# Attention exponentials: scores computed a second time by key in place of transposed exponentials

## The chip, the cores and the metric

The kernel runs on one core of one Trainium2 chip. The metric is device time in microseconds (us) of one execution. Five engines work side by side, each through its own queue of instructions in order: TensorE (PE in the profile; its weight loads stand apart as PEld), VectorE (DVE), ScalarE (ACT), GpSimd (POOL) and SyncE (SP, whose queue issues most of the transfers between the chip's memories). A score that TensorE computes lands in PSUM, eight banks of 128 partitions x 2 KB; everything else lives in the SBUF or, for long, in device memory (DRAM tiles in the code).

## What is computed

Four layers in a row on x of 2048 x 640: Fourier mixing (A), sliding-window attention (B), A, B, each with a layer norm ahead and a residual. The change is in B alone:

```python
H = 32; Dh = D // H; W = 256
qkv = (x @ wqkv).reshape(B, S, 3, H, Dh) ...
scores = jnp.einsum("bhqd,bhkd->bhqk", q, k) * (Dh ** -0.5)
mask = (idx[:, None] - idx[None, :] >= 0) & (idx[:, None] - idx[None, :] < W)
scores = jnp.where(mask[None, None], scores, -1e9)
p = _softmax(scores, axis=-1)
o = jnp.einsum("bhqk,bhkd->bhqd", p, v)
return o ... @ wo
```

32 heads of 20 features; a query sees itself and the 255 keys before it.

## The kernel before

**Layers.** `spectral` (L292) is layer A, `attention` (L702) layer B; they run as A, B, A, B (L1075 to L1079). Layer A's product over the sequence is one of Strassen's form, with matrices split into two float16 parts; the change doesn't touch it but for the name of the call that issues its matmuls.

**Attention, its loop.** The sequence is cut into 16 tiles of 128 rows and 8 blocks of 256 (QB). A slot `g` (0 to 255, loop at L1034) is one tile of queries `i` and one pair of heads `p`; `place` (L883) orders them, two pairs of heads for each of a block's two tiles by turns. In slot g the program writes, in this order: `scores(g)`, other products (`run_fill`), `exps(g-1)`, `turn(g-2)`, every fourth slot one of the two parts of `values` (lags 7 and 8, VALUE_LAGS) and `back` (lag 9), and more fill. FILL gives how many ns of fill follow: 400 and 620.

**Scores (L888).** Q and K are held transposed, features on partitions: `QS[b]` and `KS[b]`, "stacks" of three float16 parts of 20 features, 60 rows for the first head of a pair (rows 0 to 59) and 60 for the second (from row 64). Four matmuls of 60 rows give 128 queries x up to 384 keys for both heads in `sp`, a PSUM tile of two banks with two buffers. The oldest and the newest 128 keys are then merged under a triangular mask in place (L906), so that 256 columns remain; their maximum is taken (L909, over c0 to 384), scaled (L911), and is the bias of the exponential (L918, ACT, one for each head).

**From query rows to key rows.** The sum over keys needs the exponentials with keys on partitions. `turn` (L922) transposes them by TensorE, four float32 transposes of 128 x 128 (L929) into `ptp`, copies them to the SBUF tile `ptq` by ACT (L935), and POOL zeroes what the window and causality exclude (L938, L940); L938 makes the oldest tile out of the merged one.

**Values and back.** `values` (L947) multiplies V by `ptq` for four heads at once, each in a quarter of TensorE's columns (L961); V has a column of ones per head, so the sum of the exponentials comes with it. DVE copies the result (L966). `back` (L968) turns it to rows (L972), divides by the sum, and splits it in two float16 parts.

**Fill.** The projections of the next block (`proj_qk` L733, `proj_v` L738, products at L275 and L750), the output product of the block before (`out_tile` L795, L806), transposes of 128 columns (L834) and, ahead of the next layer A, its first products (L195) are cut into single matmuls, which `run_fill` (L857) deals out between a slot's steps. `proj.qk` stores each finished piece to DRAM on SP's queue; after the last one of K, and again of Q, `load_stack` (L726) loads the stack of the next block in six transfers. The last tiles' output is summed by parts (`last_out`, L765).

**What sets the order.** Each engine runs its own list in order. The lists are written by a planner from the program's order and a model of times, within the data's dependences; `tc.issue_after(x)` keeps an instruction behind x on its engine. A tile with a tag and `bufs=n` has n buffers in turn: a new one waits until the buffer it gets is released by its last reader. Transfers of SP wait in SP's queue for the buffers and data that they need.

Of the kernel before, what the change touches and what calls it, by code (L numbers as in the profile page):

```python
# [14 lines left out]
OP = mybir.AluOpType  # L15
# [22 lines left out]
LAST_STEPS = (1, 257)  # L38
# [14 lines left out]
def body(ctx: ExitStack, tc: tile.TileContext, x_in, cmat, whid, wqkv, wo, out):  # L53
# [6 lines left out]
    # matrices are held as two float16 parts each  # L60
# [6 lines left out]
    # 1 where a key of the tile two before the query's is still in the window: key > query  # L67
    mask = pers.tile([P, P], I32, name="mask")
    neg = pers.tile([P, P], F32, name="neg")

    def constants():
        make_identity(nc, idf[:])
        nc.vector.tensor_copy(idh, idf)
        nc.gpsimd.memset(mask, 1)
        nc.gpsimd.memset(neg, NEG)
        nc.gpsimd.affine_select(out=mask, in_=mask, pattern=[[1, P]], base=0, channel_multiplier=-1,
                                compare_op=OP.is_gt, fill=0.0)
# [9 lines left out]
    mx_d = dram.tile([1, 2], F32, name="mxd")  # L87

    normed = [None]

    def layer_norm(xs):
        """(x - mean) / sqrt(var + eps), times X_UP, in float32, of some tiles."""
# [48 lines left out]
    # what both kinds of layers hold at some time: the matrix in use with what is read along with it,  # L141
    # and two smaller tiles that pass from the one kind to the other while the rest of it is still at work
# [9 lines left out]
    # parts of z for the seven products, in the order in which they are used  # L152
    B11, T2, B21, T3, T1, T4, B22 = range(7)

    class Hidden:
        """The product over the features, for a tile of the sequence at a time."""
# [20 lines left out]
        def stage(self, s, pool, new=new_f):  # L177
            """Yields the time of each product in ns, and 0 where a set of them is complete."""
# [9 lines left out]
            def product(c, n):  # L188
# [4 lines left out]
                for dt in range(ND):  # L193
                    for l, r in ((0, 0), (0, 1), (1, 0)):
                        self.last = nc.tensor.matmul(z[:, :HD], xt[:, l, dt], w[:, r, c, dt, cs],  # L195
# [43 lines left out]
    def fill_stack(t, b, w):  # L239
        """The three parts of a head's features one below the other, for the products of all their pairs."""  # L240
        for pi in range(2):
            for r, part in enumerate((0, 1, 0) if w == 0 else (0, 0, 1)):
                v = qk_d[b][w][part].rearrange("(p two d) t -> two d p t", two=2, d=DH)[pi]
                r0 = 64 * pi + DH * r
                load(t[r0:r0 + DH], v)

    class Projections:
        """The products with the weights of B, for a block of QB rows at a time."""
# [19 lines left out]
        def qk(self, b, w, ct):  # L268
# [4 lines left out]
            for dt in range(ND):  # L273
                for l, r in ((0, 0), (0, 1), (1, 0)):
                    nc.tensor.matmul(pf[:, :QB], self.w[l][:, dt, cols], xt[:, :, r, dt, :],  # L275
# [12 lines left out]
    # ------------------------------------------------------------------ A  # L288
    # y = [Cr | -Ci] [z_re ; z_im] with z = xn W^T. The product over the sequence is Strassen's, in Winograd's
    # form: rows in pairs of tiles, the inner dimension in its real and imaginary halves, columns in halves of HD.  # L290
    # It is summed in rounds of RS tiles of the sequence.
    def spectral(layer, res_src, hidden, first):  # L292
        with ExitStack() as st:
# [10 lines left out]
            # small pieces of work done beside the main products, one after each of them  # L304
# [36 lines left out]
            def transposed(xs, k, xt):  # L341
                pt = new_f().bitcast(F16)[:, :ND * P].rearrange("p (a b) -> p a b", a=ND)
                for dt in range(ND):
                    nc.tensor.transpose(pt[:, dt], xs[:, k, dt * P:(dt + 1) * P], idh)
# [92 lines left out]
            def product(r, bank, cc, m, start, stop):  # L437
                o = bank[:, :HD]
                n = 0
                for k in range(RS):  # L440
                    zc = hidden.zc[RS * r + k]
                    for a, b in ((0, 0), (0, 1), (1, 0)):
                        nc.tensor.matmul(o, cc[m][:, a, k * P:(k + 1) * P], zc[:, m, b],  # L443
# [87 lines left out]
            # the weights of B: their largest exponent, then the two parts  # L531
# [21 lines left out]
            def b_scale():  # L553
# [5 lines left out]
                nc.tensor.transpose(pt[:2, :P], m2, idf)  # L559
# [545 lines left out]
```

## Time and profile before

| | us |
|---|---|
| three runs | 2437.78, 2438.85, 2439.06 |
| median | 2438.85 |
| span of the profiled execution | 2439.0 |
| first attention layer in it, about | 637 to 1277 |
| second attention layer, about | 1827 to 2439 |

In the profile's groups a row reads: line, engine, operation, output <- inputs, partitions x elements of both, count | busy us, mean ns of one | idle us of the engine just before them and what ended most of it. In the chain a row is start, duration, and whose work it was. L128 is the helper that issues nearly all of SP's transfers.

### The profile page before, as it was taken

The page shows a single profiled execution, that of the slowest core. Times are in us where ns is not written, and L with a number is a line of the kernel's source. Part 1 is how long each engine was busy: PE and PEld are TensorE (multiplying, and loading weights), DVE is VectorE, ACT ScalarE, POOL GpSimd, SP SyncE. Part 2 cuts the span into 40 slices and gives each one's busy share as a digit, 9 for nine tenths or more (in the row PEclk, how much of TensorE's full clock was granted, in tenths as well). Part 3 has the DMA queues.
Part 4 walks back from the last instruction along what each step waited for, and adds up shares of the span by engine and source line. Part 5 has one row for each costly group of instructions (what it writes and reads, how often), then busy time and mean ns, then how long its engine had stood idle before and what let it go on. Part 6 is the DMA issues. An engine that isn't in the chain of part 4 may idle for free.

```text
span 2439.0 us, 53596 instructions
## 1 busy us (share of the span) xinstructions
PE 2314.2 (95%) x20577; PEld 1569.1 (64%) x20577; DVE 1884.4 (77%) x4209; ACT 1357.7 (56%) x2695; POOL 1203.0 (49%) x1448
## 2 busy tenths in 40 slices
PE   7999898987999999999989999999789999999998
PEld 5666576656656666666656777776566666666665
DVE  7888979697778777878877767576967777777776
ACT  5334444433467777777753343443326777777775
POOL 5676757564223333333446867685732233333333
PEclk9999999998999999999999999999999999999999
DMA  5755646274522323232314545355544232322210
GB/s 176 292 198 184 208 149 209 89 250 128 161 64 64 72 75 82 73 78 66 121 67 150 195 137 196 131 190 188 176 142 102 63 70 65 77 66 71 62 44 23
DMA packets 191668, 302.25 MB, mean 124 GB/s; under 512 B 14004, under 2 KB 120756, under 8 KB 182196
## 3 DMA queue, kind: packets, MB, share of 16 engines
q1 hardware_dynamic: 156564, 222.47, 30.9%
q10 hardware_dynamic: 34848, 76.36, 8.3%
q8 instruction: 161, 2.64, 0.4%
q14 instruction: 95, 0.78, 0.1%
HBM read 201.46 MB, written 97.32 MB: 122 GB/s over the span
## 4 chain that ended last, share of the span: by engine, by line
PE 72%; DVE 19%; issue 3%; DMA 3%; ACT 2%; POOL 1%; DVEq 0%; ACTq 0%; SPq 0%; POOLq 0%
PE pf L275 11%; PE ptp L929 9%; PE pv L961 9%; PE pf L195 8%; PE y L443 7%; DVE cc L427 6%; PE pf L750 5%; PE sp L903 5%; PE pf L806 5%; PE z L443 5%; PE x L443 4%; DVE res L450 2%; DVE lnst L98 1%; PE pv L972 1%; PE pf L834 1%
## 5 line engine op out<-in xcount | busy, mean ns | idle before, releaser
L443 PEld LDWEIGHTS <-cc 128*128 128x128 f16 x5376 | 527.9, 99 | 249.6 <-issue 37.2
L918 ACT ACTIVATE pn<-sp,nb,alpha 128x256 f32<-128x256 f32 (+1 forms) x1024 | 516.3, 555 | 100.0 <-DVE nb L911 80.7
L938 POOL TENSOR_SCALAR_AFFINE_SELECT ptq<-ptq 128x512 f32<-128x512 f32 x224 | 142.2, 635 | 591.5 <-ACT ptq L935 591.5
L935 ACT ACTIVATE ptq<-ptp 128x512 f32<-128x512 f32 (+1 forms) x512 | 298.7, 583 | 194.3 <-PE ptp L929 178.2
L275 PE MATMUL pf<-early,big 128*128 128x256 f16 x2400 | 343.6, 277 | 14.0 <-DVE xto L346 13.9
L909 DVE TENSOR_REDUCE m<-sp 128x2 f32<-128x512 f32 (+1 forms) x512 | 343.2, 671 | 11.7
L929 PE MATMUL ptp<-idf,pn 128*128 128x128 f32 x1984 | 314.9, 276 | 3.0 <-ACT ptq L935 0.8
L906 DVE COPY_PREDICATED sp<-mask,sp 128x256 f32<-128x256 int32 x448 | 190.5, 426 | 140.9 <-PE sp L903 131.9
L424 ACT ACTIVATE cc<-cs 128x512 f16<-128x512 f32 x256 | 151.8, 622 | 226.7 <-POOL cs L417 103.3
L443 PE MATMUL y<-zc,cc 128*128 128x320 f16 x1728 | 265.9, 301 | 11.2 <-DVE pf L450 8.1
L275 PEld LDWEIGHTS <-big 128*128 128x128 f16 x2400 | 214.1, 99 | 91.4 <-issue 65.5
L929 PEld LDWEIGHTS ptp<-idf,pn 128*128 128x128 f32 x1984 | 233.3, 141 | 37.1 <-ACT pn L918 8.7
L195 PE MATMUL pf<-big 128*128 128x320 f16 x1680 | 244.6, 301 | 9.4 <-DVE zc L209 6.5
L195 PEld LDWEIGHTS <-big 128*128 128x128 f16 x1920 | 187.5, 99 | 97.7 <-issue 18.9
L961 PE MATMUL pv<-ptq,v 128*32 128x128 f32 (+1 forms) x3840 | 243.4, 333 | 0.2
L427 DVE SCALAR_TENSOR_TENSOR cc<-cs,cc 128x512 f16<-128x512 f32 x256 | 234.6, 930 | 1.6 <-ACT cc L424 1.6
L940 POOL TENSOR_SCALAR_AFFINE_SELECT ptq<-ptq 128x512 f32<-128x512 f32 x256 | 164.0, 641 | 100.5 <-ACT ptq L935 90.6
L427 DVE SCALAR_TENSOR_TENSOR cc<-cq,cc 128x512 f16<-128x512 f32 x192 | 203.8, 1063 | 0.0
L443 PE MATMUL z<-zc,cc 128*128 128x320 f16 x1152 | 180.0, 301 | 8.6 <-DVE res L450 8.6
L443 PE MATMUL x<-zc,cc 128*128 128x320 f16 x1152 | 183.6, 304 | 2.9 <-DVE zc L209 2.9
L750 PE MATMUL pf<-big,early 128*128 128x320 f16 x960 | 170.4, 301 | 0.2
L961 PEld LDWEIGHTS pv<-ptq,v 128*32 128x32 f32 x3840 | 105.5, 109 | 91.1 <-issue 47.8
(136 smaller groups left out, 3565.6 us busy)
## 6 DMA issues: line engine op xcount, KB each, us to landing
cq<-in_cmat_dram SPq DMA_DIRECT2D x64, 1024.0 KB
accd<-res ACTq DMA_DIRECT2D x96, 320.0 KB
res<-accd SPq DMA_DIRECT2D x96, 320.0 KB
qkd<-early SPq DMA_DIRECT2D x160, 128.0 KB
ks<-qkd SPq DMA_DIRECT2D x108, 160.0 KB
qs<-qkd SPq DMA_DIRECT2D x84, 160.0 KB
x2d<-res ACTq DMA_DIRECT2D x32, 320.0 KB
xtd<-xto ACTq DMA_DIRECT2D x32, 320.0 KB
```

Source lines behind the costliest of these rows:

```text
L195: self.last = nc.tensor.matmul(z[:, :HD], xt[:, l, dt], w[:, r, c, dt, cs], start=k == 0, stop=k == 14).ins
L275: nc.tensor.matmul(pf[:, :QB], self.w[l][:, dt, cols], xt[:, :, r, dt, :], start=k == 0, stop=k == 14)
L427: nc.vector.scalar_tensor_tensor(cc[m][:, 1], f, C_UP, cc[m][:, 0], op0=OP.mult, op1=OP.subtract)
L443: nc.tensor.matmul(o, cc[m][:, a, k * P:(k + 1) * P], zc[:, m, b], start=start and n == 0, stop=stop and n == 3 * RS - 1, skip_group_check ...
L750: nc.tensor.matmul(pf[:, :320], proj.rows[b][0][:, ti, l, dt, :], proj.w[r][:, dt, cols], start=k == 0, stop=k == 14)
L906: nc.vector.copy_predicated(sp[:, :, 2 * P:3 * P], mask[:, None, :].to_broadcast([P, 2, P]), far)
L909: nc.vector.tensor_reduce(m, sp[:, :, c0:3 * P], axis=AX.X, op=OP.max)
L918: nc.scalar.activation(pn[:, pi, c0 - P:], sp[:, pi, c0:3 * P], AF.Exp, bias=nb[:, pi:pi + 1], scale=alpha[:, 0:1])
L929: nc.tensor.transpose(pt[:, pi, a], pn[:, pi, a * P:(a + 1) * P], idf)
L935: nc.scalar.activation(q[:, h:h + 2, a0 + 1 + first:a0 + 3], pt[:, :, first:], AF.Copy)
L940: ins = nc.gpsimd.affine_select(out=q[:, :, a0 + 2], in_=q[:, :, a0 + 2], pattern=[[0, 4], [1, P]], base=0, channel_multiplier=-1, compare ...
L961: nc.tensor.matmul(pv[32 * h:32 * h + 32, cols], VS_[kt][:, VS * hh:VS * hh + 32], q[:, h, sel], start=kt == j, stop=kt == j + 1, tile_pos ...
```

## The change

The maxima are still found from scores by query (`scores`, without the scaling L911). But the exponentials are not: the maxima of eight slots (SHARE) are transposed by one small TensorE transpose, split into two float16 parts, stored to DRAM, and loaded as two more rows under each head's 60 rows of Q (`hand_on`). K's stack gets two rows of the constant 2^15 there, loaded from a DRAM tile of ones. A second product of 62 rows with K and Q in the other roles (`by_key`) so gives scores minus maximum, with keys on partitions, for all three tiles of keys, and one ACT instruction writes sigmoid(alpha x - 20) from PSUM to `ptq`; both products and sums of V then carry the same factor. The float32 transposes, their copies and the pairs of exponentials go.

In slot g the order is now: `scores(g)`, `by_key(g-13)`, every fourth slot both parts of `values` (lag 18) and `back` (lag 20), one stretch of fill of FILL[g % 4] ns, and every eighth slot `hand_on` (lag 8; its loads one slot later). Within attention each TensorE instruction is kept behind the one traced before it, so that the planner doesn't move it. `sp` and the new `tp` have two banks and one buffer each (before: `sp` two buffers, `ptp` one bank). The copies of V and of the sums of V pass from DVE to ACT. Both stacks of a block are loaded after the last projection of Q.

```diff
-FILL = (400, 620, 1600)
...
-VALUE_LAGS = (7, 8)
-BACK_LAG = 9
+FILL = (1250, 1450, 300, 1450)
+FILL_END = 1600
...
+SHARE = 8
+HAND_LAG = 8
+KEY_LAG = 13
+VALUE_LAG = 18
+BACK_LAG = 20
+M_UP = 2.0 ** 15
+SHIFT = -20.0
...
+    def tensor(what, *args, **kw):
+        with ExitStack() as order:
+            if in_turn[0] and latest[0] is not None:
+                order.enter_context(tc.issue_after(latest[0]))
+            i = getattr(nc.tensor, what)(*args, **kw)
+        latest[0] = i.ins
+        return i
...
             for r, part in enumerate((0, 1, 0) if w == 0 else (0, 0, 1)):
                 v = qk_d[b][w][part].rearrange("(p two d) t -> two d p t", two=2, d=DH)[pi]
                 r0 = 64 * pi + DH * r
                 load(t[r0:r0 + DH], v)
+            if w:
+                load(t[64 * pi + 3 * DH:64 * pi + 3 * DH + 2], ones_d.rearrange("a (p t) -> a p t", p=NP))
...
             def proj_qk(b, w, ct):
                 yield from proj.qk(b, w, ct)
-                if ct == ND - 1:
-                    load_stack(b, w)
+                if ct == ND - 1 and w == 0:
+                    load_stack(b, 1)
+                    load_stack(b, 0)
...
-                nc.vector.tensor_scalar(o, pf[:, :320].rearrange("p (h e) -> p h e", e=DH), 32.0 / (X_UP * W_UP),
-                                        None, op0=OP.mult)
+                nc.scalar.activation(o, pf[:, :320].rearrange("p (h e) -> p h e", e=DH), AF.Copy,
+                                     scale=32.0 / (X_UP * W_UP))
...
-                sp = ps.tile([P, 2, 512], F32, tag="s", name="sp", bufs=2)
+                sp = ps.tile([P, 2, 512], F32, tag="s", name="sp")
...
-                nc.vector.tensor_reduce(m, sp[:, :, c0:3 * P], axis=AX.X, op=OP.max)
-                nb = sb.tile([P, 2], F32, tag="nb", name="nb", bufs=4)
-                nc.vector.tensor_scalar(nb, m, alpha[:, 1:2], None, op0=OP.mult)
-                SP_[g] = (sp, nb, c0)
+                if g % SHARE == 0:
+                    TOP[g // SHARE] = sb.tile([P, 2, SHARE // 2, 2], F32, tag="m", name="m", bufs=2)
+                nc.vector.tensor_reduce(TOP[g // SHARE][:, i % 2, p % (SHARE // 2)], sp[:, :, c0:3 * P], axis=AX.X, op=OP.max)
+
+            def hand_on(n):
+                b, k = divmod(n, 2 * NP // SHARE)
+                pf = new_f()[:2 * SHARE, :P]
+                transpose(pf, TOP.pop(n).rearrange("p i a b -> p (i a b)"), idf)
+                hl = sb.tile([2 * SHARE, 2, P], F16, tag="hl", name="hl", bufs=2)
+                nc.scalar.activation(hl[:, 0], pf, AF.Copy, scale=-1.0 / M_UP)
+                nc.vector.scalar_tensor_tensor(hl[:, 1], pf, -1.0 / M_UP, hl[:, 0], op0=OP.mult, op1=OP.subtract)
+                load(top_d[n], hl)
+                yield
+                v = top_d[n].rearrange("(i p two) a t -> two a p i t", i=2, two=2)
+                ps_ = slice(SHARE // 2 * k, SHARE // 2 * (k + 1))
                 for pi in range(2):
-                    nc.scalar.activation(pn[:, pi, c0 - P:], sp[:, pi, c0:3 * P], AF.Exp, bias=nb[:, pi:pi + 1],
-                                         scale=alpha[:, 0:1])
+                    r0 = 64 * pi + 3 * DH
+                    for i in range(2):
+                        load(QS[b][r0:r0 + 2, ps_, i * P:(i + 1) * P], v[pi][:, :, i])
...
+            def by_key(g):
...
-                pt = pp.tile([P, 2, 2, P], F32, tag="pt", name="ptp")
-                for pi in range(2):
-                    for a in range(first, 2):
-                        nc.tensor.transpose(pt[:, pi, a], pn[:, pi, a * P:(a + 1) * P], idf)
+                tp = ps.tile([P, 2, 512], F32, tag="t", name="tp")
+                for a in range(first, 3):
+                    kt = i - 2 + a
+                    k0 = (kt % 2) * P
+                    for pi in range(2):
+                        r = slice(64 * pi, 64 * pi + 3 * DH + 2)
+                        matmul(tp[:, pi, a * P:(a + 1) * P], KS[kt // 2][r, p, k0:k0 + P], QS[b][r, p, t0:t0 + P],
+                                         start=True, stop=True)
...
-                nc.scalar.activation(q[:, h:h + 2, a0 + 1 + first:a0 + 3], pt[:, :, first:], AF.Copy)
+                nc.scalar.activation(q[:, h:h + 2, a0 + first:a0 + 3],
+                                     tp[:, :, first * P:3 * P].rearrange("p a (b c) -> p a b c", c=P), AF.Sigmoid,
+                                     bias=shift, scale=alpha[:, 0:1])
...
-                    nc.vector.tensor_copy(PVS[n], pv[:, :2])
+                    nc.scalar.activation(PVS[n], pv[:, :2], AF.Copy)
...
-                run_fill(FILL[0])
-                if 0 <= g - 1 < NG:
-                    exps(g - 1)
-                if 0 <= g - 2 < NG:
-                    turn(g - 2)
+                if 0 <= g - KEY_LAG < NG:
+                    by_key(g - KEY_LAG)
...
-                run_fill(FILL[1])
+                run_fill(FILL[g % 4] if g < NG else FILL_END)
+                n, m = divmod(g - HAND_LAG, SHARE)
+                if m == 0 and 0 <= n < NG // SHARE:
+                    handed = hand_on(n)
+                    next(handed)
+                if m == 1 and 0 <= n < NG // SHARE:
+                    next(handed, None)
```

More of the change, by code (lines that the diff above doesn't have):

```diff
@@ L69, in body @@
     neg = pers.tile([P, P], F32, name="neg")
+    shift = pers.tile([P, 1], F32, name="shift")
+    ones = pers.tile([P, 2 * NP * QB // P], F16, name="ones")
     def constants():
@@ L75, in constants @@
         nc.gpsimd.memset(neg, NEG)
+        nc.gpsimd.memset(shift, SHIFT)
+        nc.gpsimd.memset(ones, M_UP)
+        nc.sync.dma_start(ones_d.rearrange("a (b c) -> (a b) c", c=2 * NP * QB // P), ones)
         nc.gpsimd.affine_select(out=mask, in_=mask, pattern=[[1, P]], base=0, channel_multiplier=-1,
@@ L87, in body @@
     mx_d = dram.tile([1, 2], F32, name="mxd")
+    ones_d = dram.tile([2, NP * QB], F16, name="onesd")
+    top_d = [dram.tile([2 * SHARE, 2, P], F16, name=f"topd{i}") for i in range(NT * NP // SHARE)]
     normed = [None]
+    in_turn, latest = [False], [None]
+    def tensor(what, *args, **kw):
[5 more added lines that the diff above has]
+        return i
+    matmul, transpose = partial(tensor, "matmul"), partial(tensor, "transpose")
     def layer_norm(xs):
@@ L558, in b_scale @@
                 pt = new_f()
-                nc.tensor.transpose(pt[:2, :P], m2, idf)
+                transpose(pt[:2, :P], m2, idf)
                 mr = sb.tile([2, 1], F32, name="mr")
@@ L879, in flush @@
                     fill.remove(u)
[L881 removed]
+            TOP, PT = {}, {}
             def place(g):
@@ L971, in back @@
                 for m in range(2):
-                    nc.tensor.transpose(pv[:, 2 + m], t[:, m], idf)
+                    transpose(pv[:, 2 + m], t[:, m], idf)
                 pbv = pv[:, 2:].rearrange("p m (h e) -> p (m h) e", e=32)
@@ L993, in back @@
                         lastd[1] = last_out(2 * b + m, lastd[0], done)
-                        fill.insert(at, (max(now[0] + LAST_STEPS[0], LAST_STEPS[1] if done < ND else 0), lastd[1], 1))
+                        fill.insert(at, (max(now[0] + LAST_STEPS[0], NG + KEY_LAG if m else LAST_STEPS[1] if done < ND else 0), lastd[1], 1))
                     lastd[0] = done
@@ L1033, in attention @@
             NG = NT * NP
-            for g in range(NG + 10):
+            for g in range(NG - 3 + BACK_LAG):
                 now[0] = g
@@ L1051, in attention @@
                     scores(g)
-                run_fill(FILL[0])
-                if 0 <= g - 1 < NG:
-                    exps(g - 1)
-                if 0 <= g - 2 < NG:
-                    turn(g - 2)
-                if g == VALUE_LAGS[0]:
+                if 0 <= g - KEY_LAG < NG:
+                    by_key(g - KEY_LAG)
+                if g == VALUE_LAG:
                     while any(u[2] < 0 for u in fill) or (unit[0] and unit[0][2] < 0):
                         run_fill(100)
-                for part in range(2):
-                    n, m = divmod(g - VALUE_LAGS[part], 4)
-                    if m == 0 and 0 <= n < NG // 4:
+                n, m = divmod(g - VALUE_LAG, 4)
+                if m == 0 and 0 <= n < NG // 4:
+                    for part in range(2):
                         values(n, part)
```

45 lines of the change are left out of this document (19 added, 26 removed).

## Prediction

> **What bounds the kernel now.** I read the busy shares first, then the chain of work that ended last, on the page of the profile.
>
> ```profile
> span 2439.0 us, 53596 instructions
> ...
> PE 2314.2 (95%) x20577; PEld 1569.1 (64%) x20577; DVE 1884.4 (77%) x4209; ACT 1357.7 (56%) x2695; POOL 1203.0 (49%) x1448
> ...
> PE 72%; DVE 19%; issue 3%; DMA 3%; ACT 2%; POOL 1%; DVEq 0%; ACTq 0%; SPq 0%; POOLq 0%
> PE pf L275 11%; PE ptp L929 9%; PE pv L961 9%; PE pf L195 8%; PE y L443 7%; DVE cc L427 6%; PE pf L750 5%; PE sp L903 5%; PE pf L806 5%; PE z L443 5%; PE x L443 4%; DVE res L450 2%; DVE lnst L98 1%; PE pv L972 1%; PE pf L834 1%
> ```
>
> TensorE (PE) is the busiest engine and most of the chain; the transposes that the change removes (L929) are 9% of the chain. But these are averages over two kinds of layers, so I took the two attention layers alone, as windows (us, then busy us and instruction count of PE, its weight loads, VectorE (DVE), ScalarE (ACT), GpSimd (POOL), then the granted clock):
>
> ```profile
> 637.00:1277.00 640.00, 628.39 (x6424) 407.58 (x6421) 504.64 (x1354) 451.28 (x911) 235.66 (x416) 1.00 0.30 80
> 1827.00:2439.00 612.00, 603.37 (x6163) 386.88 (x6161) 446.51 (x1118) 429.53 (x861) 203.04 (x390) 1.00 0.26 64
> 800.00:1200.00 400.00, 397.75 (x4269) 264.49 (x4271) 324.24 (x873) 291.07 (x574) 150.75 (x275) 1.00 0.32 85
> 1950.00:2350.00 400.00, 400.00 (x4257) 264.03 (x4258) 294.74 (x732) 286.23 (x562) 136.79 (x272) 1.00 0.28 68
> ```
>
> PE has no gap worth naming in the steady part (398 and 400 of 400 us, clock 1.00), DVE stands at 81 and 74%, ACT at 73 and 72%. A busy PE could still be a pipelined one that waits, so I looked at the chain in order of time over a few slots:
>
> ```profile
> 901.62 0.68 PE pf L806 x5
> 902.30 0.27 PE sp L903 x4
> 902.57 0.51 PE pf L806 x3
> 903.09 0.44 PE ptp L929 x4
> 903.52 0.79 PE pv L961 x16
> 904.31 0.65 PE pf L806 x4
> 904.96 0.27 PE sp L903 x4
> ```
>
> The pieces join end to end: PE is the bound here, and what its work costs is read off these rows. A 320-column product takes 0.68 / 5 = 0.136 us. Three after the scores take 0.51, four after the sums of V take 0.65: each 0.10 more than 0.136 apiece. So leaving a group that uses the array in halves (scores) or quarters (sums) costs 0.10; I take the same for entering one, which lies inside the 0.27 and 0.79.
>
> **The change, part by part.** *Transposes out.* The page's group is
>
> ```profile
> L929 PE MATMUL ptp<-idf,pn 128*128 128x128 f32 x1984 | 314.9, 276 | 3.0 <-ACT ptq L935 0.8
> ```
>
> 1984 at 0.44 / 4 = 0.11 us is 218 us of PE time: minus 218.
>
> *Scores by key in.* 16 pairs of heads, 1 + 2 + 14 x 3 = 45 tiles of keys, two halves, two layers: 2880 matmuls of 128 columns on 62 rows. Like the scores they lie in two halves of the array. Before has such pairs: this slot's first pair starts at 902.24, and two windows that end 3 ns apart show when the third matmul comes; beside it five full transposes of 128 columns:
>
> ```profile
> 902.24 0.23 PE L903 MATMUL sp<-ks,qs 60*128 60x128 f16 x2
> 902.24 0.34 PE L903 MATMUL sp<-ks,qs 60*128 60x128 f16 x3
> 936.31 0.28 PE pf L834 x5
> ```
>
> The window to 902.301 holds two matmuls, the one to 902.304 three: a pair, with new weights for both halves, lasts some 0.067 us. 1440 pairs give plus 96 us. Lower bound 0.28 / 5 = 0.056 a pair, 81 us; upper bound, if the halves ran one after the other, 0.134, 193 us. I take 96, the row with the same form.
> The Trainium skill (TensorE: Matmul & The Clock Gate, Back-to-back issue gap) speaks against this: a stream of weight load and matmul is given some 81 ns each at 128 columns. The 0.056 of L834 above is such a stream and disagrees; by that page of the skill, with no overlap of halves, the step would be 2880 x 0.081 = 233 us (an estimate).
>
> *Changes of the array's division.* Now the scores and the scores by key of another slot stand together, once in four slots the sums follow at once, and their two parts follow each other. Per four slots there were 4 + 2 groups with two changes each, 12; there will be 9. 128 x 3 x 0.10 = minus 38. At each layer's start and end 13 slots have only one kind: 2 x 13 groups with 2 changes more, plus 5. The 64 small transposes of the maxima (0.11): plus 7.
>
> PE in all: -218 + 96 - 38 + 5 + 7 = **-148 us**. The other products are the same; new amounts of FILL only move them between slots.
>
> *DVE and ACT.* First layer, 800 to 1200 us, and two of ACT over the whole run:
>
> ```profile
> L909 DVE TENSOR_REDUCE m<-sp 128x2 f32<-128x512 f32 x166 | 114.1, 687 | 3.4
> L906 DVE COPY_PREDICATED sp<-mask,sp 128x256 f32<-128x256 int32 x166 | 70.4, 424 | 46.9 <-PE sp L903 46.1 <-ACT ptq L935 0.2
> L911 DVE TENSOR_SCALAR nb<-m,alpha 128x2 f32<-128x2 f32 x165 | 49.5, 300 | 2.6
> L966 DVE COPY pvs<-pv 128x256 f32<-128x256 f32 x41 | 17.3, 422 | 6.0 <-PE pv L961 5.8
> L756 DVE TENSOR_SCALAR v<-pf 128x320 f32<-128x320 f32 x20 | 9.7, 485 | 0.7 <-PE pf L750 0.6
> L918 ACT ACTIVATE pn<-sp,nb,alpha 128x256 f32<-128x256 f32 x960 | 490.9, 562 | 98.8 <-DVE nb L911 80.4 <-DVE lnt L112 3.9 <-DVE r L983 2.9
> L918 ACT ACTIVATE pn<-sp,nb,alpha 128x128 f32<-128x128 f32 x64 | 25.6, 458 | 1.2 <-DVE nb L911 0.3
> L935 ACT ACTIVATE ptq<-ptp 128x512 f32<-128x512 f32 x480 | 286.5, 597 | 182.7 <-PE ptp L929 166.8 <-POOL ptq L940 6.6 <-PE pv L972 3.0
> ```
>
> 166 slots in 400 us: 2.41 us a slot. DVE has 324.24 / 166 = 1.95 of it; L911, L966 and L756 leave (0.30 + 0.10 + 0.06), the low part of the handed maxima adds some 0.05: 1.54. The sigmoid isn't in the trace. An exponential with the same pointers grows by 562 - 458 = 104 ns per 128 columns, so 768 columns cost 0.562 + 4 x 0.104 = 0.98 us, in place of two exponentials and a copy (over 1.5 us): ACT gets about half a microsecond a slot, which pays for the copies it takes over (0.38 to 0.44 each, one or two per four slots). Bounds 0.60 (a plain copy of 512) and 1.6 (what it replaces). Neither end makes ACT the bound of a slot of 2.1.
>
> *One bank pair each.* sp had two buffers, now one, and tp has one. The next scores wait for this slot's maximum:
>
> ```profile
> 902.68 0.43 DVE L906 COPY_PREDICATED sp<-mask,sp 128x256 f32<-128x256 int32 x1 [0.50 <-PE sp L903]
> ```
>
> Scores at 902.24, mask at 902.68, 0.43, then the maximum's 0.69, and some 0.1 back to PE: 1.7 us. The PE slot becomes 2.41 - 148 / 512 = 2.12. The slack is 0.4; the other DVE work, 1.54 - 0.42 - 0.69 = 0.43 a slot, runs between the maximum and the next mask, covered by PE's products. If all of it got in the way, 1.7 + 0.43 = 2.13, just the bound; bursts of the layer norm hurt. By key: 0.2 + 0.3 + 0.98 + 0.1 = 1.6, the same cover. PE's queue is in order already and only the order written differs, so pinning costs what stands behind these two waits: scores by key, sums and all products. Bounds 0 and 0.15 a slot; I take 0.03, plus 15.
>
> *The handed maxima.* New path, on 64 groups of 8 slots: transpose, ACT part, DVE part, store, four loads.
>
> ```profile
> 2101.03 0.36 SPq L128 DMA_DIRECT2D qkd<-early  x1
> 2102.96 1.17 SPq L128 DMA_DIRECT2D qs<-qkd  x3
> ...
> q1 hardware_dynamic: 2216, 1.10, 52.5%
> ...
> 2110.00:2112.00 2.00, 2.00 (x27) 1.31 (x26) 1.66 (x4) 1.10 (x3) 0.21 (x1) 1.00 0.28 56
> 2112.00:2114.00 2.00, 2.00 (x19) 1.42 (x18) 1.29 (x5) 0.87 (x3) 0.00 (x0) 1.00 0.00 0
> ```
>
> A load that needs the store before it is issued 1.93 us after it, and loads follow at 1.17 / 3 = 0.39. So 0.28 + 0.38 + 0.42 (nearest rows of transpose, ACT and DVE copies) + 1.93 + 4 x 0.39 + another 1.9 to land = 6.5; behind a sigmoid and a maximum 8.2. The scores by key need them 5 slots on, behind the fill of slot 8: 4 x 2.12 + 0.27 = 8.7. Hidden, by 0.5 to 2.2 us. But they share SP's queue with stores that wait for projections and with the stacks, now twelve 160 KB loads in a row at the end of the Q projections (plus small ones for the ones). The six of before moved 1.10 MB between 2102.96 and 2111 (the row of the queue from 2102 to 2112; in the windows the share of busy DMA engines, last but one, falls to 0.28 and then 0); twelve are some 15 us of queue. I take plus 10, bounds 0 and the slow rival below.
>
> *The ends.*
>
> ```profile
> 2417.67 0.34 PE L903 MATMUL sp<-ks,qs 60*128 60x128 f16 x4
> 2435.05 0.55 DVE x L781
> ```
>
> From the last scores to the end are 21 us now. Then 13 slots by key still follow, at 1.6 us or more; PE's work in them is in the sum already, what it can't fill I put at 8 us a layer (bounds 0 and 13 x 1.6 = 21), plus 16. The tiles of K are held until then, so the next spectral layer gets room for its matrices later, and SP's first transfers may stand behind the memset of ones: plus 6.
>
> Sum: 2439 - 148 + 15 + 10 + 16 + 6 = **2322**. The profiled execution (2439.0) is within 0.2 us of the median, 2438.85; no correction.
>
> **The rivals.** *Slower: the maxima arrive late.* If SP holds the hand-on behind the stacks or a waiting store, the pinned PE stands still at the scores by key, and nothing else can run. It decides from (2439 - 2322) / 64 = 1.8 us per group, or 8 per block of 32 slots on 14 blocks. A group caught behind the twelve loads is late by their 15, plus some 3 for its own loads, less the cover of 8: 14 x 10 = 140 in place of the 10 above, so 2452; if further groups are late too, more. For it: 0.5 us of slack at worst, 15 us of queue. Against: the hand-on falls every 8 slots, 17 us, so most miss the stacks.
> *The single bank binds.* DVE's bursts cost 0.15 a slot, 77 us in place of 15: 2384. For it 1.54 of 2.12; against, most of it fits behind the maximum.
> *Nothing is given back but the ends' least:* 2439 - 148 + 5 = 2296.
> *It doesn't do what it says:* the pairs by key don't overlap, plus 97: 2419, and with more per matmul up to no gain; against it the 0.067 of a pair.
> By the 81 ns of the Trainium skill, named above, that case would be at 2322 + 233 - 96 = 2459.
>
> **How the numbers follow.** Forecast 0.46, with its own range 2290 to 2370; full gain 0.14; single bank 0.13; no overlap 0.07 (0.04 of it within the noise, 0.03 slower); late maxima 0.20. A measurement of this kernel tells about 0.2%, 5 us, from no change. So faster 0.46 + 0.14 + 0.13 = 0.73, same 0.04, slower 0.23. The range 2290 to 2475 leaves out a part of the full gain and the worst of the late maxima.
>
> **What would show it.** After: some 180 to 190 slots in 400 us in the same stretch of attention (now 166); L929 gone and matmuls by key at 0.067 a pair behind the scores; 0.10 between groups only where the division changes; no row of PE waiting for DMA of qs; a sigmoid of about 1 us. I'm wrong if PE waits for qs (late maxima), for the maximum L909 (single bank), or if a slot's six take over 0.3 us.

## The result, and the profile after

The changed kernel takes 2503.59 us (median of 4 runs, 2497.84 to 2506.18) where the kernel before takes 2438.95: a ratio of 1.0262, with a 95% interval of 1.0247 to 1.0276. It is 65 us slower; the forecast was 117 us faster, 2322. The profiled execution has a span of 2503.9 us.

From the page, the span, the busy shares and the engines' shares in the chain of work that ended last:

```profile
span 2503.9 us, 54171 instructions
...
PE 2183.3 (87%) x21537; PEld 1496.5 (60%) x21537; DVE 1721.8 (69%) x3569; ACT 1153.7 (46%) x1928; POOL 1195.8 (48%) x1450
...
PE 49%; DVE 10%; DMA 3%; issue 2%; SPq 2%; ACT 2%; POOL 0%; DVEq 0%; ACTq 0%; POOLq 0%
```

TensorE (PE) is busy for 131 us less (2314.2 before), and the kernel is slower all the same: PE has stopped being the bound. Where, windows show. Each attention layer is cut at its last product of scores by query; columns are us, PE's busy us and instructions, granted clock, DMA share, GB/s. First before, then after:

```profile
637.50:1247.40 609.90, 603.52 (x6220) 1.00 0.30 79
1247.40:1300.00 52.60, 42.21 (x325) 0.94 0.29 103
1827.70:2417.70 590.00, 586.97 (x6018) 1.00 0.26 66
2417.70:2439.00 21.30, 15.69 (x144) 0.98 0.09 32
sum 1273.80, PE 1248.39; mean PE 312.10
```

```profile
626.20:1257.40 631.20, 531.29 (x6575) 0.94 0.28 78
1257.40:1311.00 53.60, 39.56 (x393) 0.84 0.20 71
1855.10:2456.10 601.00, 514.98 (x6357) 0.92 0.26 67
2456.10:2503.00 46.90, 32.59 (x337) 0.83 0.06 22
sum 1332.70, PE 1118.42; mean PE 279.61
```

Over the four stretches PE works 130 us less and stands still for 1332.7 - 1118.4 = 214 us in place of 1273.8 - 1248.4 = 25. Nearly all of the new idle time lies in the two loops (100 and 86 us), and the granted clock there is 0.94 and 0.92, not 1.00. The waits of the whole run name what PE stands for (us in total, times, longest):

```profile
PE sp L111 <- DVE m L937: 64.3, 64, 2.2
...
PE tp L111 <- DMA qs<-topd: 60.6, 10, 6.7
```

Both things that the forecast called signs of being wrong are there: waits for the maximum (L937, L909 before) on the one buffer of scores, and waits for the handed maxima. Weight loads have waits of their own beside these; I go by PE's rows.

The chain around one late group of maxima, in the second layer:

```profile
2191.91 2.85 DMA qkd<-early
...
2195.16 0.40 SPq L154
...
2196.48 1.20 SPq L154
...
2197.72 1.39 SPq L154
...
2200.78 5.04 DMA qs<-topd
...
2205.86 0.48 PE tp L111 x5
2206.34 3.05 PE pf L111 x11
```

and SyncE's queue in the same stretch, from its timeline:

```profile
2189.91 0.32 SPq L154 DMA_DIRECT2D topd<-hl  x1
...
2192.34 1.31 SPq L154 DMA_DIRECT2D ks<-qkd  x3
...
2194.84 4.27 SPq L154 DMA_DIRECT2D qs<-qkd  x6
2199.15 2.21 SPq L154 DMA_DIRECT2D qs<-topd  x4
```

The store of the maxima is issued at 2189.9 and their first load at 2199.15, 9.2 us later, behind loads of the stacks and the last store of the projections. The last of the four loads is issued at 2200.8 and lands 5.0 us later. The scores by key start at 2205.5, and PE has stood for 5 us. That costs more than the 5 us, as windows over the same place show:

```profile
2196.00:2206.00 10.00, 3.72 (x42) 0.94 0.62 108
2206.00:2211.00 5.00, 5.00 (x38) 0.50 0.02 3
2211.00:2216.00 5.00, 5.00 (x68) 0.94 0.00 0
```

After the stall the granted clock is 0.50 for 5 us, and PE gets through 38 instructions in place of 68.

### The profile page after: what moved, and what is told of

Read it like the earlier page. It is cut to its first block, busy times and chain, and to the rows that moved or that the text cites. A ratio compares the mean times of both kernels' runs of the same rounds, so it can differ in the third digit from the quotient of the medians.

```text
span 2503.9 us, 54171 instructions
## 1 busy us (share of the span) xinstructions
PE 2183.3 (87%) x21537; PEld 1496.5 (60%) x21537; DVE 1721.8 (69%) x3569; ACT 1153.7 (46%) x1928; POOL 1195.8 (48%) x1450
## 4 chain that ended last, share of the span: by engine, by line
PE 49%; DVE 10%; DMA 3%; issue 2%; SPq 2%; ACT 2%; POOL 0%; DVEq 0%; ACTq 0%; POOLq 0%
PE pf L111 23%; PE pv L111 8%; PE y L111 5%; PE sp L111 4%; PE z L111 3%; PE x L111 3%; PE tp L111 3%; SPq L154 2%; DVE cc L455 2%; DMA qs<-topd 1%; DVE m L937 1%; DVE sp L933 1%; PE acc L111 1%; ACT ptq L975 1%; DVE lnst L124 1%
## 5 line engine op out<-in xcount | busy, mean ns | idle before, releaser
L975 ACT ACTIVATE ptq<-tp,shift,alpha 128x768 f32<-128x768 f32 (+2 forms) x512 | 486.7, 951 | 351.4 <-PE tp L111 328.7
L111 PEld LDWEIGHTS <-big 128*128 128x128 f16 x4320 | 415.6, 100 | 166.4 <-issue 46.2
L937 DVE TENSOR_REDUCE m<-sp 128x2 f32<-128x512 f32 (+1 forms) x512 | 344.7, 673 | 15.8
L111 PE MATMUL pf<-early,big 128*128 128x256 f16 x2400 | 312.9, 280 | 19.7 <-DVE xto L374 15.1
L111 PE MATMUL tp<-qs,ks 62*128 62x128 f16 x2688 | 160.7, 224 | 74.2 <-DMA qs<-topd 60.6
L111 PE MATMUL sp<-ks,qs 60*128 60x256 f16 (+1 forms) x1792 | 157.7, 255 | 55.6 <-DVE m L937 51.3
L111 PEld LDWEIGHTS <-ks 62*128 62x128 f16 (+1 forms) x3008 | 123.4, 98 | 133.8 <-issue 71.1
L111 PE MATMUL pv<-ptq,v 128*32 128x128 f32 (+1 forms) x3840 | 201.1, 353 | 0.0
L149 POOL TENSOR_TENSOR xs<-lny,xs 128x640 f16<-128x640 f32 x63 | 96.5, 1534 | 139.9 <-ACT xs L148 134.1
L111 PEld LDWEIGHTS pv<-ptq,v 128*32 128x32 f32 x3840 | 114.3, 117 | 66.0 <-issue 17.8
```

The source lines that it names most:

```text
L111: i = getattr(nc.tensor, what)(*args, **kw)
L149: eng.tensor_tensor(lo, y, hi, op=OP.subtract)
L937: nc.vector.tensor_reduce(TOP[g // SHARE][:, i % 2, p % (SHARE // 2)], sp[:, :, c0:3 * P], axis=AX.X, op=OP.max)
L975: nc.scalar.activation(q[:, h:h + 2, a0 + first:a0 + 3], tp[:, :, first * P:3 * P].rearrange("p a (b c) -> p a b c", c=P), AF.Sigmoid, bia ...
```

## The experiments

Three theories stood at the start: the late maxima are the cost (the first theory, T1), the pinned order is (T2), or the single buffer of the scores (the third, S in the later runs). The turns of the output joined them after e2. All edits are to the changed kernel, unless another base is named.

**e1: no loads of maxima.** Q's two rows hold constants, loaded with the stack as K's are, so the exponentials aren't those of the reference.

```diff
-            if w:
+            if True:
                 load(t[64 * pi + 3 * DH:64 * pi + 3 * DH + 2], ones_d.rearrange("a (p t) -> a p t", p=NP))
...
-                for pi in range(2):
-                    r0 = 64 * pi + 3 * DH
-                    for i in range(2):
-                        load(QS[b][r0:r0 + 2, ps_, i * P:(i + 1) * P], v[pi][:, :, i])
+                return
```

> The changed kernel, but the maxima are transposed, split and stored and then not loaded: Q's two extra rows are filled once per block with the same constants as K's, together with the stack. So the exponentials aren't those of the reference. Theory 1 (late maxima: the loads stand in SP's queue behind the twelve loads of the stacks or behind a load of x2 that waits for an earlier store; PE stops at the scores by key, and then runs at a lower clock for some us): per block of 32 slots some 10 us go in the second layer (slot 21 of the block) and some 13 in the first (slots 20 and 29), six blocks each, so about 138 us of 2503.6: 2365, range 2340 to 2395, no slot over 5 us in the middle blocks. Theory 2 (the pinned order costs, wherever something is late) and theory 3 (the single bank of the scores, through VectorE): nothing much changes, 2460 or more.

Measured: 2444.87 us, ratio to before 1.0023 [1.0013, 1.0033], between the two expectations. The late maxima cost 59 us, and without their loads the change still gains nothing. The largest wait of PE that is left here is for the scores' buffer:

```profile
PE sp L111 <- DVE m L937: 74.5, 67, 2.8
...
PE tp L111 <- ACT ptq L971: 11.7, 12, 1.2
```

**e2: the maxima on ScalarE's queue**, their loads a slot later.

```diff
-                load(top_d[n], hl)
+                nc.scalar.dma_start(top_d[n], hl)
...
-                        load(QS[b][r0:r0 + 2, ps_, i * P:(i + 1) * P], v[pi][:, :, i])
+                        nc.scalar.dma_start(QS[b][r0:r0 + 2, ps_, i * P:(i + 1) * P], v[pi][:, :, i])
...
-                if m == 1 and 0 <= n < NG // SHARE:
+                if m == 2 and 0 <= n < NG // SHARE:
```

> The changed kernel, with the store and the four loads of the maxima issued on ScalarE's queue in place of SP's, the loads one slot later, so that they stand behind no stack and no load of x2. Theory 1: nearly all of the stall goes, 2370 to 2400; what is left is transfers that share the sixteen DMA engines and the issue time on ScalarE (5 x 0.3 us per eight slots). Theories 2 and 3: 2460 or more, since the order of PE and the banks are the same.

Measured: 2481.42 us, 1.0180 [1.0164, 1.0197]; 22 us better, far less than expected, and 37 us above e1. PE hardly waits for maxima any more (0.5 us). But ScalarE now stands in its own order behind the stores it issues (its sigmoid waits 16.6 us for them), and PE's wait for the copies named `early`, which free a fill buffer, is 27.5 us in place of e1's 10.7; how the 37 us divide isn't shown. One slot in each block of the first layer still takes 8 to 9 us. The timeline of one:

```profile
902.89 0.44 PE L111 MATMUL pf<-idh,os 128*128 128x128 f16 x5 [1.05 <-DVE early L312]
904.13 0.44 PE L111 MATMUL pf<-idh,os 128*128 128x128 f16 x5 [0.79 <-ACT ot L868]
905.15 0.44 PE L111 MATMUL pf<-idh,os 128*128 128x128 f16 x5 [0.58 <-DVE ot L866]
906.38 0.49 PE L111 MATMUL pf<-idh,os 128*128 128x128 f16 x5 [0.79 <-ACT ot L868]
```

These are the four turns of a block's output. `back` runs all four in one go when it opens the next block's output tile (`for g in moves: list(g)`), ahead of their due slots. They pass through the two fill buffers, so each waits for a copy by ScalarE or VectorE (DVE). The same line is in the kernel before; there the planner could put other products between, here the written order holds.

**e3: not pinned.**

```diff
-            in_turn[0] = True
+            in_turn[0] = False
```

> The changed kernel without the pin: the planner may move PE's instructions in attention, as before the change. Theory 2 (the pinned order is the cost): 2420 or less. Theory 1: the planner's order is fixed ahead of the run as well and its model of times doesn't know the late transfers, so 2460 to 2520, with PE still waiting for the loads of the maxima.

Measured: 2577.07 us, 1.0565 [1.0544, 1.0586]. The pin as a whole is no loss: without it the kernel is 73 us slower still. T2 falls, but T1's expectation (2460 to 2520, PE still waiting for the maxima) is missed too: no row of PE waits for `topd` any more. What has grown is PE's own work:

```profile
PE 2317.4 (90%) x21537; PEld 1510.4 (59%) x21537; DVE 1713.1 (67%) x3569; ACT 1146.3 (45%) x1928; POOL 1201.7 (47%) x1450
```

That is 134 us more than the changed kernel's 2183.3 for as many products at the same mean clock (0.953 and 0.950), while PE's idle time falls by 63 us. The planner deals single products in between scores, scores by key and sums: counted in PE's timelines (800 to 1200 and 1950 to 2300 us), the division of the array changes 3.57 and 3.35 times a slot here, 2.14 and 2.09 times in the changed kernel, 3.13 and 3.05 times before. At the 0.10 us of the prediction that makes some 70 of the 134 us, an estimate; the rest is open.

**e4: Q projected before K, each stack loaded after its own projections.**

```diff
-                if ct == ND - 1 and w == 0:
-                    load_stack(b, 1)
-                    load_stack(b, 0)
+                if ct == ND - 1:
+                    load_stack(b, w)
...
-                for w in (1, 0):
+                for w in (0, 1):
```

> The changed kernel with Q projected before K and each stack loaded behind its own projections, so two bursts of six loads (plus the rows of ones) in place of one of twelve. Theory 1: the stall at the stacks shrinks from some 10 us per block to 2 to 5, that behind the load of x2 in the first layer stays: 2430 to 2470. Theories 2 and 3: unchanged, 2495 to 2510.

Measured: 2480.51 us, 1.0169 [1.0148, 1.0189]. Six loads in a row in place of twelve are worth 23 us, as much as a queue of their own in e2, but less than expected: PE's wait for the maxima falls from 60.6 to 16.8 us, and its wait for the sigmoid grows from 12.6 to 30.7.

**e5: nothing reads the scores.** e1, and the mask, the maximum and the hand-on are left out as well; the score products stay.

```diff
-                nc.vector.copy_predicated(sp[:, :, 2 * P:3 * P], mask[:, None, :].to_broadcast([P, 2, P]), far)
...
-                nc.vector.tensor_reduce(TOP[g // SHARE][:, i % 2, p % (SHARE // 2)], sp[:, :, c0:3 * P], axis=AX.X, op=OP.max)
...
-                    handed = hand_on(n)
-                    next(handed)
```

> As e1 (no loads of maxima), and nothing reads the scores by query: the mask, the maximum and the hand-on transposes are left out, the score products on PE stay. Theory S (the single buffer of the scores is what keeps e1 at 2444.9): in e1 PE was idle 43.5 us ahead of score products in the first attention loop and 45.8 us in the second; those go, with 8 us of idle and about 7 us of work of the 64 hand-on transposes and some of the half clock behind each stall, so 2320 to 2355 us. Rival (the waits only move: the same slots then wait for the sigmoid's buffer, for the turns or for the fill copies on ACT): 2400 us or more.

Measured: 2374.85 us, 0.9734 [0.9710, 0.9759]; 70 us less than e1, between the two expectations. The waits for the scores' buffer are gone, but more than half of their time comes back as waits of the scores by key for the sigmoid, which has one buffer too (11.7 us in e1):

```profile
PE tp L111 <- ACT ptq L964: 60.6, 67, 3.2
```

The run takes three things out together: the waits on the buffer, DVE's 1.1 us in each slot (mask and maximum), and the hand-on's transposes with the fill buffer that they take. The direct trial, a second buffer for the scores, wasn't run.

**e7: no mask.** e1, with the mask ahead of the maximum left out.

```diff
-                nc.vector.copy_predicated(sp[:, :, 2 * P:3 * P], mask[:, None, :].to_broadcast([P, 2, P]), far)
```

> As e1, and the mask ahead of the maximum is left out (480 instructions of 0.42 to 0.46 us on DVE), so the chain between two score products on the one buffer is 0.7 us in place of 1.1 plus the gaps; the maximum and the hand-on stay. Theory S: half or more of the 89 us of idle ahead of score products goes, 2375 to 2410 us. Rival (the stalls come from bursts of DVE's other work, layer norm above all, not from the length of the chain): the waits at slots 72/104+32k stay and the time is 2425 us or more.

Measured: 2407.63 us, 0.9876 [0.9850, 0.9903]: 37 us less than e1 for 0.42 us less in each slot's chain. The wait for the maximum falls to less than half of e1's 74.5 us, so it is the length of the chain that counts, more than bursts of other work (though leaving the mask out frees DVE as well):

```profile
PE sp L111 <- DVE m L935: 32.8, 51, 1.8
```

**e6: the turns at their due slots.** e2, without the forced run.

```diff
                 if k == 0:
-                    for g in moves:
-                        list(g)
-                    moves.clear()
                     OS[b] = sb.tile([P, 2, 2, D], F16, tag="os", name="os", bufs=2)
```

> As e2 (store and loads of maxima on ScalarE's queue, one slot later), and the four turns of a block's output are no longer run in one go four slots after they were made; they go into the stretches of other products at their due slots. Theory U (the forced burst of 20 transposes through two pf buffers is what made slot 84+32k 9 us in the first layer and 4 to 5 in the second, now that PE keeps the written order): PE's idle time ahead of these transposes, 15 + 6 us in e1, goes with the half clock behind it: 2445 to 2465 us. Rival (the turns wait for the same copies wherever they stand, or the slot is long for the stacks of K and Q): 2475 to 2490 us.

Measured: 2435.48 us, 0.9982 [0.9973, 0.9992]: 46 us less than e2, more than expected, and a hair below the kernel before. The same four stretches:

```profile
628.30:1218.20 589.90, 523.24 (x6563) 0.96 0.29 83
...
1815.90:2384.50 568.60, 507.61 (x6352) 0.95 0.26 71
...
sum 1260.80, PE 1103.96; mean PE 275.99
```

**e11: the turns alone**, with the maxima still on SyncE's queue.

> The changed kernel with one edit: the turns of a block's output at their due slots. The maxima still go on SyncE's queue. If the forced turns cost 46 us by themselves: 2450 to 2465 us. Rival (with the late maxima in the next slot of the same block they are covered, since the burst also delays the products that wait for the maxima): 2475 us or more.

Measured: 2497.79 us, 1.0240 [1.0225, 1.0255]: only 6 us less than the changed kernel, hardly clear of the noise. The rival holds. The forced burst gave the late maxima time to land; without it PE reaches the scores by key earlier and stands there longer (60.6 us in 10 waits before this edit):

```profile
PE tp L111 <- DMA qs<-topd: 71.3, 16, 7.1
```

**e10: none of the three.** The edits of e1, e5 and e6 together (not e2's).

> As e5 (no loads of maxima; mask, maximum and hand-on left out, so nothing reads the scores by query), and the turns of a block's output at their due slots as in e6. If the three losses add up (late maxima 59 us, readers of the single buffer 70, forced turns 46 off a kernel of 2503.6), 2325 to 2345 us. Rival (the turns and the late maxima share their cost, since both stall the slots 20 to 21 of a block): 2355 us or more.

Measured: 2347.09 us, 0.9626 [0.9610, 0.9642]: between the two expectations, and 28 us less than e5, so the turns cost 28 here, 46 in e2 and 6 in the changed kernel. The four stretches:

```profile
628.50:1171.90 543.40, 504.98 (x6530) 0.98 0.32 91
...
1771.20:2294.50 523.30, 487.86 (x6319) 0.97 0.29 76
...
sum 1166.30, PE 1064.11; mean PE 266.03
```

**e8: a bank of its own for the hand-on.** On e6; the transposed maxima no longer take a fill buffer, and DVE makes both parts.

```diff
-                pf = new_f()[:2 * SHARE, :P]
+                pf = ps.tile([P, 512], F32, tag="h", name="top")[:2 * SHARE, :P]
...
-                nc.scalar.activation(hl[:, 0], pf, AF.Copy, scale=-1.0 / M_UP)
+                nc.vector.tensor_scalar(hl[:, 0], pf, -1.0 / M_UP, None, op0=OP.mult)
```

> As e6, and the hand-on of the maxima gets a PSUM bank of its own in place of one of the two buffers of the fill products, and both of its parts come from DVE (ScalarE made the first, and DVE stood 34 us in all, 0.5 us each of 64, waiting for it, with the next mask queued behind). Theory D (what is left of the waits for the single buffer of scores comes from DVE standing in its order behind ScalarE, not from its own work): the 8.0 and 5.8 us that PE stands ahead of the hand-on transposes go and some of the 77 us ahead of score products: 2408 to 2427 us. Rival (these are too few and too far apart to matter): 2430 to 2440 us.

Measured: 2420.45 us, 0.9931 [0.9907, 0.9954], 15 us less than e6. The number is theory D's, the mechanism only in part: PE's wait for the maximum doesn't fall (63.3 us in e6, 68.0 here). What goes is the time that PE stood ahead of the hand-on's transposes, mostly for a fill buffer (e6, then e8):

```profile
L111 PE MATMUL pf<-idf,m 128*16 128x128 f32 x64 | 18.0, 282 | 13.8 <-DVE early L312 12.0 <-DVE lnt L138 1.0 <-DVE early L235 0.7
```

```profile
L111 PE MATMUL top<-idf,m 128*16 128x128 f32 x64 | 17.9, 279 | 0.0
```

**e9: the low parts of Q and K later.** On e8, in `proj.qk` and `scores`.

```diff
-            nc.vector.scalar_tensor_tensor(t[:, 1], pf[:, :QB], down, t[:, 0], op0=OP.mult, op1=OP.subtract)
-            load(qk_d[b][w].rearrange("a (c p) t -> c p a t", p=P)[ct], t)
+            self.late.append(low)
...
+                if proj.late:
+                    with tc.issue_after(top.ins):
+                        proj.late.pop(0)()
```

`low` holds the two lines taken out, and `top` is the slot's maximum. The loads of the stacks are put off with them.

> As e8, and the low part of each projection of Q and K (DVE, which waits for the high part on ScalarE: 64 us in 160 waits) is queued on DVE behind the next slot's maximum in place of ahead of that slot's mask. Theory D: a third to a half of what PE stands ahead of score products goes (77 us in e6), 2380 to 2412 us. Rival: the waits stay, since DVE's own bursts (layer norm, turns) and the 1.1 us of mask and maximum make them, or the products of Q and K now wait for their buffer that is freed later: 2415 us or more.

Measured: 2445.28 us, 1.0027 [1.0008, 1.0046]: 25 us worse than e8. DVE's wait for ScalarE did fall (groups by shape, e8 first, then e9), but the products that reuse the fill buffer now wait for it, 6.2 us in e8:

```profile
L312 DVE SCALAR_TENSOR_TENSOR early<-pf,early 128x256 f16<-128x256 f32 x160 | 66.9, 419 | 66.0 <-ACT early L311 62.0 <-DMA qkd<-early 2.6
```

```profile
L314 DVE SCALAR_TENSOR_TENSOR early<-pf,early 128x256 f16<-128x256 f32 x160 | 66.1, 414 | 26.7 <-ACT early L312 26.7
```

```profile
PE pf L111 <- DVE early L314: 33.2, 45, 2.1
```

The wait for the maximum hardly moved (68.0 us in e8, 60.8 in e9), so DVE standing behind ScalarE was not the main thing that held the scores.

**e12: half of the turns through the hand-on's bank**, on e8.

```diff
-                pt = new_f()
+                pt = new_f() if k or now[0] >= NT * NP else ps.tile([P, 512], F32, tag="h", name="top")
```

> As e8, and the first of the two turns of a tile takes the hand-on's bank in place of a buffer of the fill products while scores are computed. If the 13 us (first layer) and 7 us (second) that PE stands in e8 ahead of products and transposes into the two fill buffers come from the turns holding them: 2400 to 2414 us. Rival (those waits are for copies that DVE and ScalarE make late, whichever buffer is used): within 5 us of e8, 2415 to 2426 us.

Measured: 2408.57 us, 0.9877 [0.9861, 0.9894], 12 us less than e8, as its first expectation has it. This version computes all that the kernel before does and is 30 us faster than it.

## Why the prediction was wrong

**PE's work: right in sign, too small in size.** The sum of PE was to fall by 148 us. It falls by 1248.4 - 1118.4 = 130 in the changed kernel, and by 1248.4 - 1064.1 = 184 in e10, where the clock is 0.97 to 0.98; e10 lacks the hand-on transposes, which the prediction priced at 7, so some 177 at that clock. The term for the scores by key was one of those mis-sized. The chain shows an undisturbed slot of the changed kernel:

```profile
907.52 0.17 PE tp L111 x6
907.68 1.46 PE pf L111 x10
```

Three pairs in 0.17 us are 0.057 a pair, next to the lower bound of the prediction (0.056), not 0.067: 1440 x 0.010 = 14 us. The changes of the array's division, counted as in e3, fall from 3.13 and 3.05 a slot to 2.29 and 2.05 in e10: some 47 us at 0.10 each, where the term had 38. The last 6 of the 29 us between 148 and 177 are open. The halves overlap, so the fourth rival falls, and with it the estimate of 233 us by the 81 ns of the Trainium skill (TensorE: Matmul & The Clock Gate, Back-to-back issue gap): the measurement decides. Between 177 and 130 lie 47 us in which the changed kernel runs the same products longer; the windows after a stall, with half the clock, show how.

**The sigmoid: right.** 0.991 us against 0.98, from the groups by shape. (What it replaces is 2 x 0.562 + 0.597 = 1.72 us by the prediction's rows, not 1.6; nothing hangs on it.)

```profile
L975 ACT ACTIVATE ptq<-tp,shift,alpha 128x768 f32<-128x768 f32 x448 | 443.8, 991 | 313.3 <-PE tp L111 291.2 <-DVE sp L933 13.6 <-POOL ptq L982 3.2
```

**The handed maxima: the step that failed first.** "Hidden, by 0.5 to 2.2 us" took 1.93 us from store to load and 1.9 to land; measured at the end of a block are 9.2 and 5.0. The 10 us are 59 by e1. I had the right mechanism among the rivals, and had put it at 140 us alone. e2 and e4 show what it hangs on: SyncE's queue and the row of twelve stack loads. A load that waits for a store does the same. In the first layer SyncE issues nothing between the store of one group's maxima and the `x` load, which keeps the loads of the maxima behind it for 12 us (the wait rows put 9.4 us of it down to the store of `x3d` out of an `x` buffer):

```profile
998.86 0.32 SPq L154 DMA_DIRECT2D topd<-hl  x1
1010.61 0.35 SPq L154 DMA_DIRECT2D x<-x2d  x1
1011.05 1.14 SPq L154 DMA_DIRECT2D qs<-topd  x4
```

**The single buffers: mis-sized from 15 to 70 us.** e5 against e1 gives 70, with DVE's freed time, the hand-on's transposes and the buffer they take among them; e7 shows that the mask alone is worth 37. The rival's 77 us was the better size, and the "0.03 a slot" had nothing behind it but the mean slack of 0.4 us. A slot isn't the mean: PE's work in a slot varies, and with a chain of 1.7 us every short slot waits, while a long one gives nothing back. That the 0.43 us of other DVE work always fits behind the maximum was not shown, either, and the sigmoid's buffer, which I had put under the same cover, takes over when the scores' buffer lets go.

**The turns: no term at all.** "Pinning costs what stands behind these two waits" overlooked the waits inside the fill. Four turns written in one go stall a pinned PE: 28 us in e10, 46 in e2, and 6 where late maxima lie behind them. e3 shows that the pin in itself isn't the fault.

**The ends: about right.** PE's idle time in the two stretches after the last scores grows from 10.4 + 5.6 to 14.0 + 14.3 us, so 12 of the 16. Outside the four stretches the changed kernel takes 2503.9 - 1332.7 = 1171.2 us in place of 1165.2, 6 more, which is the size of the last term; but it is the net of 11 less ahead of the first loop and 16 more between the layers, so that is luck. What holding K's tiles longer costs wasn't tried by itself.

**The sum: added up wrong.** 2439 - 148 + 15 + 10 + 16 + 6 is 2338, not 2322: the 16 of the ends stands among the terms and is missing from the total. So my own terms made the change 101 us faster, not 117, and the prices of the rivals that start from 2322 belong 16 higher (late maxima 2468, single bank 2400, no overlap 2435). The slip doesn't explain the miss: 2503.6 is above all of them.

**What the terms were worth.** Taken out one after another, the late maxima are 59 of the 2503.6 (e1), the readers of the scores 70 (e5) and the turns 28 (e10): 2347. That lies 25 us above the forecast and 9 above its terms rightly added. The 9 are small by luck: by e10's windows PE's work is 184 less than before and its idle time 102.2 - 25.4 = 77 more, where the terms had 148 and 47. (2439.0 - 184.3 + 76.8 is 2331.5, and the rest to e10's span of 2341.0 lies outside the four stretches.) And e10 does without the maxima, which the changed kernel needs. How the 102 us divide between the sigmoid's buffer and other waits is open. **The rivals** were priced as alternatives, one in place of another. Late maxima and the single buffer came together, with a third cost beside them, and so the time lies above the late maxima's price and out of the range. In the same 400 us (800 to 1200) there are 154 slots, not the 180 to 190 that the forecast asked for:

```profile
L937 DVE TENSOR_REDUCE m<-sp 128x2 f32<-128x512 f32 x154 | 106.2, 690 | 4.5
```

## What to carry to other kernels

When a change takes work off an engine that was full, each wait that this work used to cover has to be priced against the shortest slot, not the mean one. The losses can come together, so the forecast for "several rivals at once" needs a number too; and a sum is worth adding up a second time from its own terms. A written order kept on an engine can make a burst in it a stall, though the order itself may be a gain (e3): look for places that run pending pieces in one go. Small transfers that a pinned engine waits for need a queue on which nothing large or waiting stands ahead of them, and when one stall goes the next slot must be looked at, because a burst may have been its cover (e11 against e6).

## What the runs showed of the hardware

A stall of 5.05 us left the granted clock at 0.50 for the next 5 us (the windows above). That such a stall halves the clock is what the Trainium skill says (TensorE: Matmul & The Clock Gate, Part 1: The HAM clock gate), which gives a window of about 3.4 us without activity. I had not expected that no single long gap is needed. In e2's burst of turns no gap is over 1.05 us, and yet, in its windows:

```profile
901.50:906.60 5.10, 1.89 (x22) 1.00 0.28 81
906.60:909.20 2.60, 2.60 (x13) 0.51 0.75 139
909.20:911.40 2.20, 2.20 (x21) 0.81 0.75 129
```

PE was busy for 1.89 of 5.10 us, in pieces, and the clock was 0.51 right after. So this burst of short waits is paid twice: as 3.2 us of idle time, and by some 1.7 us more in the products that follow (2.60 us at 0.51 and 2.20 at 0.81 of the clock, an estimate from these rows).

Also new to me: in the stack's loads the issue of one transfer on SyncE's queue went from 0.40 us to 1.20 and 1.39 in a row of six loads, and the last small load behind them took 5.0 us to land (the chain above).
